# First token block of a spectral GLU kernel: tiles 4 to 7 transposed by VectorE blocks and a way through HBM instead of by TensorE

## The chip, the cores and the metric

One core of a Trainium2 chip runs the whole program. The metric is the device time of one execution in microseconds (us), the lower the better. A core has TensorE (matrix products, written PE in the profile, its weight loads PEld), VectorE (DVE), ScalarE (ACT), GpSimd (POOL) and SyncE (SP, which here only issues transfers). They run their own instruction streams in order and wait for each other by semaphores. On-chip memory is SBUF and, for TensorE's results, PSUM in banks of 128 x 512 numbers; HBM lies outside.

## The reference, cut to what matters

The input x has 2048 tokens of 640 features, in float32. First a layer norm, a two-dimensional real FFT, a product with a complex filter, the inverse FFT, and a residual sum; then a layer norm, a bilinear GLU and a second residual sum:

```
h   = x + irfft2(rfft2(layernorm(x)) * (w_r + 1j * w_i))
z   = layernorm(h)
out = h + ((z @ w_gate) * (z @ w_up)) @ w_down        # 640 -> 1728 -> 640
```

## The kernel before

Tokens are held in 16 tiles of 128 tokens (partitions) by 640 features, `X[0]` to `X[15]`. Both Fourier transforms are matrix products with tables. The GLU works on two token blocks of 8 tiles (1024 tokens) each; a block is split into two halves `sb` of 512 tokens: tiles 0 to 3 are half 0 and tiles 4 to 7 half 1 of the first block. Every product of the GLU is done in three matmuls on rounded numbers: an operand is stored as a high part (rounded) and a low part (the rest), and high x high, high x low and low x high are summed.

The gate and up weights are cut into 14 chunks. Chunks 0 to 11 are multiplied by a Strassen scheme (`strassen`), which needs sums and differences of quarters of z (`t12`, `t34`, made of `TJ`, the differences that `turn_lo` makes, and of `TJ["b"]`, copies of tiles 0 to 3). Chunks 12 and 13 are plain products in `gu(c, sb)`; in the first block they run first, so that TensorE has work while the Strassen operands are being made.

For a product, z must lie with features on partitions: each normalised tile must be transposed. The change touches how this is done for tiles 4 to 7.

The place is the loop `for t in range(NT)` near the end of the inverse transform. Its iteration t issues, in this order:

1. `turn_mm(k)` for k in `tside[t]`: TensorE's transposes (L811) of a normalised tile.
2. `unfold(t + 2)`: ScalarE copies a part of tile t+2's PSUM (`s`, L758); `turn_hi(k)` on ScalarE (L821 the high part, L825 the copy for Strassen); VectorE's sum and difference `q` (L766, L767), among which the small scale computations in `dside[t]` are spread; `turn_lo(k)` on VectorE (L829 the low part, L834 and L835 the Strassen differences); GpSimd's sums `yt` (L763, L771).
3. `id_mm(t + 3)` on TensorE, into a pair of PSUM banks `eo`.
4. `aside[t]` on ScalarE: squares for the variance, the inverse root (L223), `normalise(k)` (L799).
5. `is1_mm(t)` on TensorE (the second half of the inverse transform), into a pair of banks, `y`, or `eo` for t = 12; and for t = 13 `gu(13, 0)` behind it, which takes banks of `eo` over.
6. `acc(t)` on VectorE: adds the result to `X[t]` (L782, or L784 with a row sum for t below 8). acc(12) is issued in iteration 13, behind L767 of tile 15.

The scale r and shift b of a tile (L223 on ScalarE; L225, L215, L227, L792 on VectorE) are computed for groups of tiles: 0 to 2, 3 to 5, 6 and 7. For 6 and 7 this ends in iteration 13; normalise(6) stands in iteration 13, normalise(7) in 14.

Behind the loop tiles 6 and 7 are transposed (`transp`), then `gu(12, 0)` runs, `load_raw(0)` (L995, SP) fetches the weights of Strassen chunk 0 into a buffer that held the inverse transform's tables, and the first step of the GLU begins (the branch `p == 6`, `blk == 0`). It issues, in an order written out by hand: t1's and t2's high parts (ScalarE, L853) with `copies` (L1006 on ScalarE splits off the high part of chunk 0's weights, L1007 on VectorE the low part); `late` (the low part of the gate of chunk 13, L948); t1's and t2's low parts (VectorE, L853); `fifth((5, 6, 7))`, TensorE's transposes of the last 128 features of tiles 5 to 7 (L842), with their high and low parts (L844, L845); the gate of chunk 12 (L954, L955, L956); sums of weights (L1010 to L1013) with high and low parts (L1018, L1023); `gu(13, 1)`, its gate (L945 to L948), `t_rest` (L849), t34 (L864, L868), `gu(12, 1)`, and then `strassen`, chunk after chunk.

The order of each engine is the order of the code; SP's queue is too: a transfer that waits holds those behind it. Later in the kernel, for the second block, VectorE already transposes tiles in 32 x 32 blocks (L1406), and they go to HBM and back (L1409, L1399).

Of the kernel before, what the change touches and what calls it, by code (L numbers as in the profile page):

```python
# [27 lines left out]
PLAIN, MID = 5, 10  # L28
IPLAIN, IFAR = 5, 9
SUMS = 7  # L30
IPARTS = ((5, 4), (9, 3), (12, 4))
AGAIN = {0: (5, 3, "dC"), 1: (8, 2, "qt"), 4: (10, 3, 0), 7: (13, 3, 1)}
NR = 4
# [16 lines left out]
def f32(ap):  # L50
    return ap.bitcast(F32)
# [29 lines left out]
def tile_spectral_glu(ctx: ExitStack, tc: tile.TileContext, x, wre, wim, wgu, wlast, wdown, wdlast,  # L81
                      cc, ci, fmain, frem, imain, irem, mm, out):
    nc = tc.nc
# [7 lines left out]
    tt, act = nc.vector.tensor_tensor, nc.scalar.activation  # L91
# [22 lines left out]
    def wk(shape, name):  # L114
        return work.tile(shape, F32, tag="wk", name=name)
# [4 lines left out]
    def mmx(o, l, r, start, stop):  # L120
        nc.tensor.matmul(o, l, r, start=start, stop=stop, skip_group_check=True)  # L121
# [108 lines left out]
    SC = {}  # L230
# [548 lines left out]
    def acc(t, ps, total=None):  # L779
        xv = X[t].rearrange("p (a b) -> p a b", a=2)  # L780
        if total is None:
            tt(xv, ps[:, :, 0:320], xv, op=OP.add)  # L782
        else:
            nc.vector.scalar_tensor_tensor(xv, ps[:, :, 0:320], 1.0, xv, op0=OP.mult, op1=OP.add, accum_out=total)  # L784
# [9 lines left out]
            SC[t] = r[:, i:i + 1], b[:, i:i + 1]  # L794
        return fs, cs

    def normalise(t, z):
        Z[t] = z
        act(z, X[t], AF.Identity, bias=SC[t][1], scale=SC[t][0])  # L799

    PT = {}

    def turn_mm(t):
        if t < 5:
            ps = pair("y").rearrange("p a b -> p (a b)")
        else:
            ps = single()
        n = 5 if t < 5 else 4
        PT[t] = ps[:, 0:n * P].rearrange("p (k s) -> p k s", k=n)
        for k in range(n):  # L810
            nc.tensor.transpose(PT[t][:, k], Z[t][:, k * P:(k + 1) * P], ident)  # L811

    def turned(t, l):
        sb, i = divmod(t % 8, 4)
        return xt[:, sb, 0:5 if t < 5 else 4, l, i * P:(i + 1) * P], PT[t]

    TJ = {}

    def turn_hi(t):
        hi, pk = turned(t, 0)  # L820
        act(hi, pk, AF.Copy)  # L821
        if t == 0:
            TJ["b"] = home("dA", [P, 4, 4, P], "bt")
        if t < 4:
            act(TJ["b"][:, t], pk[:, 0:4], AF.Copy)  # L825

    def turn_lo(t):
        lo, pk = turned(t, 1)
        tt(lo, pk, f32(turned(t, 0)[0]), op=OP.subtract)  # L829
        if t % 8 >= 4:  # L830
            j = t % 4
            d = TJ[j] = wk([P, 4, P], "tj")
            b = TJ["b"][:, j]
            tt(d[:, 0:2], pk[:, 0:2], b[:, 0:2], op=OP.subtract)  # L834
            tt(d[:, 2:4], pk[:, 2:4], d[:, 0:2], op=OP.subtract)  # L835

    def fifth(ts):
        ps = single()
        sb, i = divmod(ts[0] % 8, 4)
        n = len(ts) * P  # L840
        for k, t in enumerate(ts):
            nc.tensor.transpose(ps[:, k * P:(k + 1) * P], Z[t][:, 512:640], ident)  # L842
        hi, lo = (xt[:, sb, 4, l, i * P:i * P + n] for l in range(2))
        act(hi, ps[:, 0:n], AF.Copy)  # L844
        tt(lo, ps[:, 0:n], f32(hi), op=OP.subtract)  # L845

    def t_rest(j):
        b = TJ["b"][:, j].rearrange("p (a k) n -> p a (k n)", a=2)
# [20 lines left out]

        return [high, low]  # L870

    def transp(t):
        turn_mm(t)
        turn_hi(t)
        turn_lo(t)

    PG = {}

    def gu(c, sb, which=(1, 0), ks=range(5)):
        if which[0] == 1:  # L880
            PG[c, sb] = [single() for _ in range(2 if c < NC - 1 else 1)] * 2
        w = W[c]
        if c < NC - 1:
            wv = w.rearrange("p l (m k f) -> p l m k f", m=2, k=5)
            sel = [(PG[c, sb][m], lambda l, k, m=m: wv[:, l, m, (k + 3) % 5]) for m in which]
        else:
            wv = w.rearrange("p l (k f) -> p l k f", k=5)
            sel = [(PG[c, sb][0], lambda l, k: wv[:, l, k])]
        for b, ww in sel:
            for k in ks:  # L890
                mmx(b, ww(0, k), xt[:, sb, k, 0], k == 0, False)
                mmx(b, ww(0, k), xt[:, sb, k, 1], False, False)
                mmx(b, ww(1, k), xt[:, sb, k, 0], False, k == 4)
# [10 lines left out]
    for ts in (range(3), range(3, 6), range(6, 8)):  # L904
        n, t0 = len(ts), ts[-1] + 1
        fs, cs = scale_shift(ts, [scrap] * n, total[:, ts[0]:t0])
        dside[t0].append(fs[0])
        t1 = ts[0] + 6 if n == 3 else t0 + 3
        dside[t1] += fs[1 + n:]
        dside[t1 + 1 + (n == 2)] += cs[1:]  # L910
        for i, t in enumerate(ts):
            (behind[t1 - n + i + 3] if t in (0,) else aside[t1 - n + i]).insert(0, fs[1 + i])
            aside[t + 7 + (t == 3)].append(lambda t=t: normalise(t, zb[:, t % 4]))
            tside[t + 9].append(t)
        aside[t1].append(cs[0])

    tside[NT - 1] = []
# [41 lines left out]
    for t in range(NT):  # L959
        for k in tside[t]:  # L960
            turn_mm(k)
        if t == NT - 3:
            unfold(t + 2, [], tside[t], [lambda: acc(t - 1, PY[t - 1])])
            for f in dside[t]:
                f()
        elif t + 2 < NT:
            unfold(t + 2, dside[t], tside[t])
        else:
            for k in tside[t]:
                turn_hi(k)  # L970
                turn_lo(k)
        if t + 3 < NT:
            id_mm(t + 3)
        for f in aside[t]:
            f()
        if t == NT - 3:
            is1_mm(t)
            ht = home("qm", [P, 8192], "ht", F32R)
            hop = cut(ht, 0, 7, 2, 512)
            t3 = [cut(ht, 7168, 2, 512), home("qt", [P, 2, 512], "t3", F32R)]  # L980
            banks("a", "pglu")
            gu(NC - 1, 0)
        else:
            is1_mm(t)
        if t != NT - 4:
            acc(t, PY[t], total[:, t:t + 1] if t < 8 else None)
        if t == NT - 2:
            late = gate_parts(NC - 1, 0)
    transp(6)
    transp(7)  # L990
    gu(NC - 2, 0)
    stage = home("stage", [P, 1448], "raw")

# [221 lines left out]
    for n, (blk, p) in enumerate(steps):  # L1215
        if p == 6:
            if blk == 0:
# [1 line left out]
                copies, sums, high, low = prep(0, blk, nc.vector)  # L1219
                TJ["12"] = home("qr", [P, 2, 2, 2, 512], "t12", F32R)  # L1220
                t1s = [t12(j) for j in range(4)]
                for j in range(3):
                    t1s[j][0]()
                copies()
                t1s[3][0]()
                late()
                t1s[0][1]()
                t1s[1][1]()
                t1s[2][1]()
                fifth((5, 6, 7))  # L1230
                wdn = load_d(p)
                t1s[3][1]()
                late = gate_parts(NC - 2, 0)
                sums()
                high()
                late()
                gu(NC - 1, 1)
                late = gate_parts(NC - 1, 1)
                for j in range(4):
                    t_rest(j)  # L1240
# [332 lines left out]
```

## Time and profile before

| | |
|---|---|
| median of 3 runs | 671.34 us (671.05 to 671.4) |
| the profiled execution | 671.31 us |
| its span, first to last instruction | 669.5 us |
| busy: TensorE, VectorE, ScalarE, GpSimd | 659.8, 469.1, 321.5, 393.3 us |
| granted TensorE clock over the span | 1.00 |

Times within the profile are us from the span's start. A timeline row gives start, length, engine, line, operation, the tile written and the tile read, their shapes and a count; rows of the same kind in a row are merged, their length is from the first start to the last end. In brackets stands how long the engine had been idle before it, and which instruction ended that. `e`, `y`, `eo` and `d` are PSUM banks, `zb` the normalised tiles, `xt` the transposed operand, `wst`, `wdir` weights.

### The profile page before, as it was taken

The page shows a single profiled execution, that of the slowest core. Times are in us where ns is not written, and L with a number is a line of the kernel's source. Part 1 is how long each engine was busy: PE and PEld are TensorE (multiplying, and loading weights), DVE is VectorE, ACT ScalarE, POOL GpSimd, SP SyncE. Part 2 cuts the span into 40 slices and gives each one's busy share as a digit, 9 for nine tenths or more (in the row PEclk, how much of TensorE's full clock was granted, in tenths as well). Part 3 has the DMA queues.
Part 4 walks back from the last instruction along what each step waited for, and adds up shares of the span by engine and source line. Part 5 has one row for each costly group of instructions (what it writes and reads, how often), then busy time and mean ns, then how long its engine had stood idle before and what let it go on. Part 6 is the DMA issues. An engine that isn't in the chain of part 4 may idle for free.

```text
span 669.5 us, 10243 instructions
## 1 busy us (share of the span) xinstructions
PE 659.8 (99%) x3695; PEld 587.1 (88%) x3695; DVE 469.1 (70%) x952; ACT 321.5 (48%) x622; POOL 393.3 (59%) x377
## 2 busy tenths in 40 slices
PE   6999999999999999999999999999999999999997
PEld 6999999888888888888888899888888888888887
DVE  6969997788767767594857567754757475757644
ACT  6977774585525243453626146534434251624220
POOL 3101124750397978969686445198786869697610
PEclk9999999999999999999999999999999999999999
DMA  8639885502212120142332467212011121212004
GB/s 319 227 107 283 245 246 157 163 1 80 78 40 80 39 79 33 28 99 60 98 79 84 93 134 260 79 41 78 12 35 73 41 78 40 79 40 80 1 0 158
DMA packets 48953, 66.12 MB, mean 99 GB/s; under 512 B 24082, under 2 KB 30670, under 8 KB 48774
## 3 DMA queue, kind: packets, MB, share of 16 engines
q1 hardware_dynamic: 48246, 62.91, 30.5%
q0 software_dynamic: 288, 2.16, 0.8%
q8 instruction: 29, 0.48, 0.3%
q10 hardware_dynamic: 368, 0.39, 0.2%
q14 instruction: 22, 0.18, 0.1%
HBM read 54.61 MB, written 10.84 MB: 98 GB/s over the span
## 4 chain that ended last, share of the span: by engine, by line
PE 95%; ACT 2%; DVE 1%; DMA 1%; issue 0%; DVEq 0%
PE e L121 50%; PE d L121 26%; PE eo L121 4%; PE y L121 2%; PE re L121 2%; PE u L476 2%; PE im L527 2%; PE im L121 2%; PE im L270 2%; PE ir L527 1%; DMA x<-in_x_dram 1%; ACT s L296 1%; ACT fold L212 0%; ACT fold L211 0%; PE y L811 0%; PE u L527 0%
## 5 line engine op out<-in xcount | busy, mean ns | idle before, releaser
L121 PE MATMUL e<-xt,wst 128*128 128x512 f32 x864 | 211.0, 390 | 0.0
L121 PEld LDWEIGHTS e<-xt,wst 128*128 128x128 f32 x864 | 160.7, 188 | 31.7
L1093 DVE TENSOR_TENSOR x<-d,x 128x320 f32<-128x320 f32 x280 | 120.5, 483 | 41.2 <-PE d L121 37.0
L121 PE MATMUL d<-wd,ht 128*128 128x320 f32 x832 | 142.1, 309 | 0.0
L121 PEld LDWEIGHTS d<-wd,ht 128*128 128x128 f32 x832 | 129.6, 188 | 5.1
L1007 POOL TENSOR_TENSOR wst<-raw,wst 128x1024 fp32r<-128x1024 f32 x23 | 55.4, 2410 | 69.9 <-ACT wst L1006 69.9
L121 PE MATMUL e<-t,wst 128*128 128x512 f32 x360 | 94.1, 391 | 0.0
L121 PEld LDWEIGHTS e<-t,wst 128*128 128x128 f32 x360 | 66.6, 188 | 13.3 <-ACT h L1147 0.3
L121 PE MATMUL d<-wt,ht 128*128 128x320 f32 x360 | 68.9, 309 | 0.0
L1023 POOL TENSOR_TENSOR wst<-raw,wst 128x896 fp32r<-128x896 f32 (+1 forms) x46 | 65.1, 1436 | 0.2 <-ACT wst L1018 0.2
L121 PEld LDWEIGHTS d<-wt,ht 128*128 128x128 f32 x360 | 57.3, 188 | 0.8
L1109 ACT ACTIVATE ht<-e 128x512 fp32r<-128x512 f32 x44 | 26.4, 600 | 50.0 <-DVE e L1171 24.1
L1018 ACT ACTIVATE wst<-raw 128x896 fp32r<-128x896 f32 (+1 forms) x48 | 30.1, 676 | 30.7 <-POOL raw L1012 30.0
L1167 DVE TENSOR_TENSOR e<-e,h 128x512 f32<-128x512 f32 x24 | 16.8, 699 | 39.2 <-ACT wst L1018 21.7
L1068 DVE TENSOR_TENSOR x<-d,x 128x320 f32<-128x320 f32 x62 | 27.5, 486 | 22.6 <-PE d L121 22.6
L687 ACT ACTIVATE wd<-draw 128x320 fp32r<-128x320 f32 (+1 forms) x30 | 15.7, 560 | 55.2 <-POOL draw L697 52.3
L121 PE MATMUL e<-xt,wdir 128*128 128x512 f32 x180 | 41.9, 392 | 0.0
L1147 ACT ACTIVATE h<-e 128x512 f32<-128x512 f32 x24 | 14.3, 596 | 56.7 <-PE e L121 56.7
L121 PEld LDWEIGHTS e<-xt,wdir 128*128 128x128 f32 x180 | 33.4, 188 | 7.5 <-ACT xt L821 0.5
L1112 DVE TENSOR_TENSOR ht<-e,ht 128x512 fp32r<-128x512 f32 x54 | 37.0, 686 | 1.6 <-ACT ht L1109 1.3
L1164 ACT ACTIVATE h<-e 128x512 f32<-128x512 f32 x24 | 14.4, 598 | 46.8 <-PE e L121 46.8
L666 POOL TENSOR_TENSOR wd<-draw,wd 128x640 fp32r<-128x640 f32 x8 | 12.4, 1577 | 40.8 <-ACT wd L665 40.8
(240 smaller groups left out, 1187.1 us busy)
## 6 DMA issues: line engine op xcount, KB each, us to landing
raw<-in_wgu_dram SPq DMA_DIRECT2D x24, 640.0 KB
draw<-in_wdown_dram SPq DMA_DIRECT2D x24, 320.0 KB
wts<-in_wre_dram SPq DMA_DIRECT2D x16, 322.0 KB
x<-in_x_dram SPq DMA_DIRECT2D x15, 320.5 KB
out_dram<-x SPq DMA_DIRECT2D x15, 320.0 KB
bits<-in_mm_dram SPq DMA_DIRECT2D x32, 128.0 KB
wts<-in_wim_dram SPq DMA_DIRECT2D x9, 322.0 KB
zfar<-zr SPq DMA_DIRECT2D x32, 80.0 KB
```

The costliest lines, as they stand in the source:

```text
L121: nc.tensor.matmul(o, l, r, start=start, stop=stop, skip_group_check=True)
L527: nc.tensor.matmul(out, y[:, h, a:b], inv(g, h), start=n == 0, stop=n == len(ys) - 1)
L687: act(o[:, 0, a:a + n], src, AF.Copy)
L1007: ptt(wa[:, 1], stage[:, 0:1024], f32(wa[:, 0]), op=OP.subtract)
L1018: act(ws[:, 0, o:o + b - a], stage[:, a:b], AF.Copy)
L1023: ptt(ws[:, 1, o:o + b - a], stage[:, a:b], f32(ws[:, 0, o:o + b - a]), op=OP.subtract)
L1068: tt(xv, ps[b][:, 0:320], xv, op=OP.add)
L1093: tt(xv, o, xv, op=OP.add)
L1109: act(hop[:, a, 0], src, AF.Copy)
L1112: engine.tensor_tensor(hop[:, a, 1], src, f32(hop[:, a, 0]), op=OP.subtract)
L1164: act(h1, oa, AF.Copy)
L1167: tt(ob, ob, h1, op=OP.add)
```

## The change

Tiles 0 to 3 are handled as before. For tiles 4 to 7:

- `normalise` writes its 640 features in another order: of each group of 160 features, five by 32, the blocks of 32 are brought together in such a way that a later copy can fetch whole runs.
- normalise(6) and (7) stand one iteration earlier (12 and 13), and so do the scale and shift of tiles 6 and 7 (iteration 12).
- `swap(ts)`, called at the end of iterations 11 (tile 4), 12 (tile 5) and 13 (tiles 6 and 7): VectorE transposes the tile in 32 x 32 blocks; SP writes it to HBM (320 KB, one transfer a tile); and SP reads it back in four transfers a tile, one for each group of 32 partitions, so that the blocks land where a full transpose would have them.
- `land_hi(t)` (ScalarE) makes the high part from that, `land_lo(t)` the low part on GpSimd and the two Strassen differences on VectorE. They are issued in iteration 14 for tile 4, in 15 for tile 5, and in the first GLU step for tiles 6 and 7.
- TensorE's transposes of tiles 4 to 7 and of the fifths, with their high and low parts, are gone.
- The first GLU step issues in another order, and `gu(13, 1)` runs all matmuls that need high parts of z first, then those that need low parts.

```diff
+SWAPS = {11: (4,), 12: (5,), 13: (6, 7)}
...
-    def normalise(t, z):
+    def normalise(t, z, mixed=False):
         Z[t] = z
-        act(z, X[t], AF.Identity, bias=SC[t][1], scale=SC[t][0])
+        i = X[t]
+        if mixed:
+            i, z = i.rearrange("p (k q b) -> p k q b", k=5, q=4), z.rearrange("p (q k b) -> p k q b", k=5, q=4)
+        act(z, i, AF.Identity, bias=SC[t][1], scale=SC[t][0])
...
     def turn_lo(t):
         lo, pk = turned(t, 1)
         tt(lo, pk, f32(turned(t, 0)[0]), op=OP.subtract)
-        if t % 8 >= 4:
-            j = t % 4
-            d = TJ[j] = wk([P, 4, P], "tj")
-            b = TJ["b"][:, j]
-            tt(d[:, 0:2], pk[:, 0:2], b[:, 0:2], op=OP.subtract)
-            tt(d[:, 2:4], pk[:, 2:4], d[:, 0:2], op=OP.subtract)
-
-    def fifth(ts):
...
+    zround = far.tile([4, P, D], F32, name="zround")
+    ZR, ZL = {}, {}
+
+    def swap(ts):
+        for t in ts:
+            r = ZR[t] = wk([P, D], "zs")
+            nc.vector.transpose(r, Z[t])
+        for t in ts:
+            nc.sync.dma_start(zround[t - 4], ZR[t])
+        for t in ts:
+            o = wk([P, D], "zl")
+            ZL[t] = o.rearrange("p (i k b) -> p k i b", i=4, k=5)
+            src = zround[t - 4].rearrange("(i a) (q x) -> q a i x", i=4, q=4)
+            for q in range(4):
+                nc.sync.dma_start(o[32 * q:32 * q + 32].rearrange("p (i x) -> p i x", i=4), src[q])
+
+    def split4(ap):
+        return ap.rearrange("p k (i b) -> p k i b", i=4)
+
+    def land_hi(t):
+        act(split4(xt[:, 1, :, 0, (t - 4) * P:(t - 3) * P]), ZL[t], AF.Copy)
+
+    def land_lo(t):
+        hi, lo = (xt[:, 1, :, l, (t - 4) * P:(t - 3) * P] for l in range(2))
+        nc.gpsimd.tensor_tensor(split4(lo), ZL[t], split4(f32(hi)), op=OP.subtract)
+        j = t - 4
+        d = TJ[j] = wk([P, 4, P], "tj")
+        tt(split4(d[:, 0:2]), ZL[t][:, 0:2], split4(TJ["b"][:, j, 0:2]), op=OP.subtract)
+        tt(split4(d[:, 2:4]), ZL[t][:, 2:4], split4(d[:, 0:2]), op=OP.subtract)
...
-    def gu(c, sb, which=(1, 0), ks=range(5)):
+    def gu(c, sb, which=(1, 0), ks=range(5), late=False):
...
+            if late:
+                for l, m in ((0, 0), (1, 0), (0, 1)):
+                    for k in ks:
+                        mmx(b, ww(l, k), xt[:, sb, k, m], l + m + k == 0, m == 1 and k == 4)
+                continue
...
-        dside[t1 + 1 + (n == 2)] += cs[1:]
+        dside[t1 + 1] += cs[1:]
         for i, t in enumerate(ts):
             (behind[t1 - n + i + 3] if t in (0,) else aside[t1 - n + i]).insert(0, fs[1 + i])
-            aside[t + 7 + (t == 3)].append(lambda t=t: normalise(t, zb[:, t % 4]))
-            tside[t + 9].append(t)
+            aside[t + 7 + (t == 3) - (n == 2)].append(lambda t=t: normalise(t, zb[:, t % 4], t >= 4))
+            if t < 4:
+                tside[t + 9].append(t)
...
         if t != NT - 4:
             acc(t, PY[t], total[:, t:t + 1] if t < 8 else None)
+        if t in SWAPS:
+            swap(SWAPS[t])
+        if t >= NT - 2:
+            land_hi(t - 10)
+            land_lo(t - 10)
         if t == NT - 2:
             late = gate_parts(NC - 1, 0)
-    transp(6)
-    transp(7)
     gu(NC - 2, 0)
...
                 t1s = [t12(j) for j in range(4)]
-                for j in range(3):
-                    t1s[j][0]()
+                t1s[0][0]()
+                t1s[1][0]()
+                land_hi(6)
                 copies()
-                t1s[3][0]()
+                land_hi(7)
                 late()
+                land_lo(6)
                 t1s[0][1]()
                 t1s[1][1]()
+                land_lo(7)
+                t1s[2][0]()
+                t1s[3][0]()
                 t1s[2][1]()
-                fifth((5, 6, 7))
                 wdn = load_d(p)
                 t1s[3][1]()
                 late = gate_parts(NC - 2, 0)
                 sums()
                 high()
                 late()
-                gu(NC - 1, 1)
+                gu(NC - 1, 1, late=True)
```

More of the change, by code (lines that the diff above doesn't have):

```diff
@@ L795, in scale_shift @@
         return fs, cs
-    def normalise(t, z):
+    def normalise(t, z, mixed=False):
         Z[t] = z
-        act(z, X[t], AF.Identity, bias=SC[t][1], scale=SC[t][0])
+        i = X[t]
+        if mixed:
+            i, z = i.rearrange("p (k q b) -> p k q b", k=5, q=4), z.rearrange("p (q k b) -> p k q b", k=5, q=4)
+        act(z, i, AF.Identity, bias=SC[t][1], scale=SC[t][0])
     PT = {}
     def turn_mm(t):
[L804 to L810, printed above, removed]
+        PT[t] = pair("y").rearrange("p a b -> p (a b)")[:, 0:D].rearrange("p (k s) -> p k s", k=5)
+        for k in range(5):
             nc.tensor.transpose(PT[t][:, k], Z[t][:, k * P:(k + 1) * P], ident)
     def turned(t, l):
-        sb, i = divmod(t % 8, 4)
-        return xt[:, sb, 0:5 if t < 5 else 4, l, i * P:(i + 1) * P], PT[t]
+        return xt[:, 0, :, l, t * P:(t + 1) * P], PT[t]
     TJ = {}
@@ L823, in turn_hi @@
             TJ["b"] = home("dA", [P, 4, 4, P], "bt")
-        if t < 4:
-            act(TJ["b"][:, t], pk[:, 0:4], AF.Copy)
+        act(TJ["b"][:, t], pk[:, 0:4], AF.Copy)
     def turn_lo(t):
@@ L829, in turn_lo @@
         tt(lo, pk, f32(turned(t, 0)[0]), op=OP.subtract)
-        if t % 8 >= 4:
-            j = t % 4
-            d = TJ[j] = wk([P, 4, P], "tj")
-            b = TJ["b"][:, j]
-            tt(d[:, 0:2], pk[:, 0:2], b[:, 0:2], op=OP.subtract)
-            tt(d[:, 2:4], pk[:, 2:4], d[:, 0:2], op=OP.subtract)
-    def fifth(ts):
[L838 to L845, printed above, removed]
+    zround = far.tile([4, P, D], F32, name="zround")
[23 more added lines that the diff above has]
+        tt(split4(d[:, 2:4]), ZL[t][:, 2:4], split4(d[:, 0:2]), op=OP.subtract)
     def t_rest(j):
@@ L870, in t34 @@
         return [high, low]
[L872 to L875, printed above, removed]
     PG = {}
-    def gu(c, sb, which=(1, 0), ks=range(5)):
+    def gu(c, sb, which=(1, 0), ks=range(5), late=False):
         if which[0] == 1:
@@ L909, in tile_spectral_glu @@
         dside[t1] += fs[1 + n:]
-        dside[t1 + 1 + (n == 2)] += cs[1:]
+        dside[t1 + 1] += cs[1:]
         for i, t in enumerate(ts):
             (behind[t1 - n + i + 3] if t in (0,) else aside[t1 - n + i]).insert(0, fs[1 + i])
-            aside[t + 7 + (t == 3)].append(lambda t=t: normalise(t, zb[:, t % 4]))
-            tside[t + 9].append(t)
+            aside[t + 7 + (t == 3) - (n == 2)].append(lambda t=t: normalise(t, zb[:, t % 4], t >= 4))
+            if t < 4:
+                tside[t + 9].append(t)
         aside[t1].append(cs[0])
-    tside[NT - 1] = []
     raw0 = home("dA", [P, 3, D], "raw0")
@@ L967, in tile_spectral_glu @@
             unfold(t + 2, dside[t], tside[t])
[L968 to L971, printed above, removed]
         if t + 3 < NT:
```

## The prediction

> **What bounds the kernel now.** I read the page first, for the engine with no room, and then the timeline of each engine around the change (140 to 180 us).
>
> ```profile
> PE 659.8 (99%) x3695; PEld 587.1 (88%) x3695; DVE 469.1 (70%) x952; ACT 321.5 (48%) x622; POOL 393.3 (59%) x377
> PEclk9999999999999999999999999999999999999999
> PE 95%; ACT 2%; DVE 1%; DMA 1%; issue 0%; DVEq 0%
> ```
>
> TensorE is busy 99% of the span and carries 95% of the chain that ended last. Behind the change it never idles again, so what it loses there arrives at the end undiminished, and so does what it saves. Its timeline through the change (start, length; the pitch is the distance between starts):
>
> ```profile
> 147.81 1.28 PE L121 MATMUL eo<-yt,tab 128*128 128x320 f32 x4
> 148.92 0.71 PE L811 MATMUL y<-ident,zb 128*128 128x128 f32 x5
> 149.47 1.24 PE L121 MATMUL y<-yt,tab 128*128 128x320 f32 x4
> 150.70 3.65 PE L121 MATMUL e<-xt,wdir 128*128 128x512 f32 x15
> 154.19 0.60 PE L811 MATMUL e<-ident,zb 128*128 128x128 f32 x4
> 154.62 2.32 PE L121 MATMUL y<-yt,tab 128*128 128x320 f32 x8
> 156.78 1.04 PE L811 MATMUL e<-ident,zb 128*128 128x128 f32 x8
> 157.57 7.21 PE L121 MATMUL e<-xt,wdir 128*128 128x512 f32 x30
> 164.62 0.49 PE L842 MATMUL e<-ident,zb 128*128 128x128 f32 x3
> 164.87 10.47 PE L121 MATMUL e<-xt,wdir 128*128 128x512 f32 x45
> 175.18 1.52 PE L121 MATMUL e<-xt,wst 128*128 128x512 f32 x6
> 176.54 1.52 PE L121 MATMUL e<-t,wst 128*128 128x512 f32 x6
> ```
>
> In order: is1_mm(12), tile 4's transposes, is1_mm(13), gu(13,0) at 150.70, tile 5's, is1_mm(14) and (15), tiles 6 and 7, gu(12,0), the fifths, gu(13,1) with gu(12,1), and the first Strassen products.
>
> **What it removes.** The four L811/L842 groups, by the distance to the next start: 0.55 + 0.43 + 0.79 + 0.25 = 2.0 us. That is the most that can be won: 669.3.
>
> **What it adds on VectorE at once.** A block transpose of a 128x640 tile is in the trace, much later:
>
> ```profile
> L1406 DVE STREAM_TRANSPOSE zr<-z x8: 834/836/845, 291.9 to 369.9; 128x640 f32<-128x640 f32 x8
> ```
>
> 0.84 us, with a pitch near 0.77. Tile 4's goes between acc(11) and the unfolding of tile 14. VectorE there, and the two ScalarE rows that matter:
>
> ```profile
> 146.69 0.48 DVE L766 TENSOR_TENSOR q<-eo,s 128x322 f32<-128x322 f32 x1
> 147.09 0.48 DVE L767 TENSOR_TENSOR q<-eo,s 128x322 f32<-128x322 f32 x1
> 147.72 0.82 DVE L829 TENSOR_TENSOR xt<-y,xt 128x640 fp32r<-128x640 f32 x1
> 148.93 0.49 DVE L766 TENSOR_TENSOR q<-eo,s 128x322 f32<-128x322 f32 x1 [0.38 <-ACT s L758]
> 149.34 0.48 DVE L767 TENSOR_TENSOR q<-eo,s 128x322 f32<-128x322 f32 x1
> 149.74 0.82 DVE L782 TENSOR_TENSOR x<-eo,x 128x640 f32<-128x640 f32 x1
> ```
>
> ```profile
> 147.57 0.92 ACT L799 ACTIVATE zb<-x,b,r 128x640 f32<-128x640 f32 x1
> 148.39 0.44 ACT L758 ACTIVATE s<-eo 128x322 f32<-128x322 f32 x1
> ```
>
> *Step 1.* L767 of tile 14 ends at 148.3 instead of 147.57. is1_mm(12) writes into the pair of banks that L767 frees, so it starts near 148.45 instead of 147.81: 0.6 lost, just what dropping tile 4's transposes gives back (0.55). TensorE is through is1_mm(13) at 150.7, as now.
>
> *Step 2.* gu(13,0) starts now at 150.70, 0.14 after acc(12) (149.74 + 0.82) ends: it waits for it. acc(12) stands behind L766/L767 of tile 15 on VectorE, these wait for ScalarE's copy s (L758, the 0.38 above), and s now has normalise(6) ahead of it in ScalarE's order, as the change puts both normalise(5) and normalise(6) into iteration 12. normalise(6) needs its scale and shift, which VectorE makes after L829 of tile 3: w and times first, L829 at about 148.65, r at 149.4, b. r has a trap:
>
> ```profile
> 142.12 0.75 POOL L771 TENSOR_TENSOR yt<-q 128x318 f32<-128x318 f32 x1
> 142.19 0.69 DVE L227 SCALAR_TENSOR_TENSOR r<-w,r 128x3 f32<-128x3 f32 x1
> ```
>
> An instruction on three columns took 0.69 and ended as GpSimd's did. The same pair of GpSimd sums runs here until about 150.0 (two of 0.75 behind 148.4). So b is ready near 150.4, normalise(6) runs to 151.2 (0.82 pitch by the two rows above), s to 151.7, L766 and L767 (0.41 each) to 152.5, acc(12) to 153.3, gu(13,0) starts at 153.5: 2.8 later than now. What was hidden is now in line. Behind it tile 5 gives back 0.43, tiles 6 and 7 0.79, the fifths 0.25, and the wait inside gu(12,0) 0.2 (30 matmuls at 0.229, the pitch of the 45, need 6.9, not 7.05): TensorE alone stands 1.2 later at gu(13,1).
>
> **The way through HBM.** All of it is issued by SP, in order: write 4, four reads 4, write 5, four reads 5, writes 6 and 7, eight reads, and only then load_raw(0), which now is issued at 156.97. Each read group waits for its write to land, and holds everything behind it. Prices:
>
> ```profile
> 108.37 0.58 SPq L718 DMA_DIRECT2D ifar<-qr  x1
> 110.78 0.30 SPq L726 DMA_DIRECT2D xt<-ifar  x1
> ```
>
> ```profile
> 175.95 0.33 SPq L995 DMA_DIRECT2D raw<-in_wgu_dram  x1
> ```
>
> ```profile
> 179.74 1.06 ACT L1006 ACTIVATE wst<-raw 128x1024 fp32r<-128x1024 f32 x1 [0.17 <-DMA raw<-in_wgu_dram]
> ```
>
> ```profile
> L1399 SPq DMA_DIRECT2D z<-zfar x16: 302/427/599, 390.2 to 402.5; - x16
> ```
>
> From a write's issue to the read that waited for it: 2.4. From the issue of 640 KB of weights to the ScalarE instruction that waited for them: 3.8. Issue of a comparable read: 0.30 to 0.60, I take the median, 0.42. When a tile's last read lands no row shows: between 2.4 and 3.8 from its issue; I take 2.4, as 80 KB is nearer the small one. Then: write 4 at 147.6 (transpose done), reads 150.0 to 151.7; write 5, reads 154.1 to 155.8; writes 6 and 7; reads 158.2 to 161.5; weights issued at 161.5, there at 165.3. Tiles 6 and 7 land at 161.9 and 163.5: ahead of the weights. The dearest thing on this path is thus not the tiles but the weights behind them.
>
> **What is late next.**
>
> ```profile
> 161.52 1.04 ACT L1006 ACTIVATE wst<-raw 128x1024 fp32r<-128x1024 f32 x1
> ```
>
> ```profile
> 160.07 0.42 DVE L834 TENSOR_TENSOR tj<-e,bt 128x256 f32<-128x256 f32 x1
> ...
> 162.59 1.23 DVE L1007 TENSOR_TENSOR wst<-raw,wst 128x1024 fp32r<-128x1024 f32 x1 [0.26 <-ACT wst L1006]
> ...
> 166.38 0.55 DVE L845 TENSOR_TENSOR xt<-e,xt 128x384 fp32r<-128x384 f32 x1
> ```
>
> ```profile
> 175.63 0.58 ACT L954 ACTIVATE u<-e 128x512 f32<-128x512 f32 x1
> ```
>
> L1006 moves from 161.52 to 165.3, **3.8**. land_hi(7) is queued behind it on ScalarE (to 167.0), so gu(13,1) starts near 167.0, not 164.87. On VectorE L1007 heads a gapless row (t1 and t2 low parts, the gate, the sums, t_rest) that ends in t34's high parts and then L954, which frees the bank for the product at 176.54: 0.3 of slack only. Into this row the change puts the differences of tiles 6 and 7 (four of 0.42, formerly ahead of L1007) and takes L845 out (0.5): **1.2**. And the low parts on GpSimd meet it:
>
> ```profile
> 181.60 2.41 POOL L1007 TENSOR_TENSOR wst<-raw,wst 128x1024 fp32r<-128x1024 f32 x1
> ```
>
> ```profile
> 182.27 2.82 DVE L859 TENSOR_TENSOR xt<-bt,xt 128x1024 fp32r<-128x1024 f32 x1 [3.14 <-ACT xt L859]
> ```
>
> Of the same size as VectorE's L1007 (1.23), it took 2.82, ending 1.08 after GpSimd's. The Trainium skill (GPSIMD Engine Reference, "8. Key points") says that GpSimd shares its SBUF interfaces with VectorE, in contention with instructions of two SBUF inputs; this trace agrees, 2.82 against 1.23. A low part takes 2.41 x 640/1024 = 1.5; tile 7's runs from 167.6 to 169.1 and stands before tile 6's difference, due at 168.2: **0.9** (bounds: 0 and 1.5). TensorE's 1.2 and its wait for land_hi(7) run beneath this.
>
> Two edits I cost at nothing. The new order of gu(13,1) keeps its 15 matmuls; the ten that need high parts only take 2.3 and cover tile 7's low part (1.5). normalise with blocks reordered and the high parts from strided blocks get the price of plain 128x640 instructions; no row shows these patterns, and half a microsecond each would still be inside the range.
>
> Sum: 3.8 + 1.2 + 0.9 = 5.9 us. The profiled execution took 671.31 (span 669.5, 1.8 around it) beside a median of 671.34: 671.3 + 5.9 = **677.2**. Its own range: with 0.30 per read SP is 1.9 earlier and ScalarE's own order then holds L1006 at about 163.4, 3.9 in all, 675.2; with 0.60, 2.9 more, 680.1.
>
> **The rivals.** *A, hidden after all:* the transfers land before they are asked for and the order on ScalarE costs nothing, so 2.0 are won: **669.3**. For it: tiles 4 to 7 aren't read by TensorE before 164, over 10 us after the first normalise. Against it: the wait of gu(13,0) for acc(12), which has no slack now. *B, only the order:* SP is quick, GpSimd disturbs nobody. gu(13,0) is then 2.3 late (r without its 0.5), the gate behind it 2.3 - 0.43, ScalarE has one high part of 0.5 less before L1006: that is 1.4 late, with the 1.2 of the differences 2.6: **673.9**. *C, the clock:* TensorE would stand still for about 4 us before the product now at 176.54 (ready near 178.6, started near 182.5). If its granted clock fell to half there, 15 matmuls at 0.229 would cost 3.4 more: **680.6**. Against it: the clock row shows no slice below 9, though TensorE waits in the first slices of the span. The Trainium skill (TensorE: Matmul & The Clock Gate, "Why this matters for your kernels") warns of idle gaps over about 3 us; no stall here is so long, so no run here shows it. *D, one tensor:* if the slots of zround were held as one, write 5 and writes 6 would also wait for the reads before them to land, 2.0 each (2.4 less the 0.42 of its issue): 4.0 more, **681.2**. Between A and B a gain and a loss may cancel: about 671.
>
> **How the numbers follow.** Forecast 0.55; B 0.18; A 0.08; C 0.08; D 0.06; cancelling 0.05. About 0.2% (1.3 us) is what a measurement of this kernel can tell from no change. Faster is A, 0.08; same is the cancelling case, 0.05; slower the rest, 0.87. The range leaves out A, the cancelling case and D, 0.19: from 673.5, just under B, to 680.7, just over C.
>
> **What would show it.** Step 1: is1_mm(12) starts near 148.4. Step 2: normalise(6) ends after 150.5 ahead of s, acc(12) ends and gu(13,0) starts near 153.4. The HBM way: SP's load_raw(0) issued after 159, with all sixteen reads ahead of it, and L1006 waiting for a DMA. The row on VectorE: L1007 after 165, a difference of tile 6 that takes over 1 us beside GpSimd's low part, TensorE idle for some 4 us before the first product with t. It is wrong if gu(13,0) starts before 151.5, or if load_raw(0) is issued before 158.5 and L1006 doesn't wait for it.

## The result, and the profile after

| | before | changed |
|---|---|---|
| median | 671.37 us (671.05 to 671.45) | 679.55 us (678.02 to 680.09) |
| the profiled execution, its span | 671.31, 669.5 us | 680.09, 678.3 us |
| granted TensorE clock over the span | 1.00 | 0.995 |

The ratio is 1.0118, with a 95% interval of 1.0106 to 1.013: slower by 8.2 us. The forecast was 677.2, with a range of 673.5 to 680.7.

The page of the changed kernel, its engines, the granted clock in 40 slices, and the chain that ended last:

```profile
PE 662.4 (98%) x3675; PEld 588.1 (87%) x3675; DVE 469.2 (69%) x951; ACT 321.8 (47%) x621; POOL 400.2 (59%) x381
PEclk9999999998999999999999999999999999999999
PE 92%; ACT 2%; DMA 2%; DVE 2%; SPq 1%; issue 1%; POOL 0%; POOLq 0%; ACTq 0%; DVEq 0%
```

TensorE has 20 instructions fewer and 2.6 us more busy time. Its share of the chain fell from 95 to 92%, and one slice of the clock row shows an 8. TensorE's timeline through the change:

```profile
148.48 1.31 PE L122 MATMUL eo<-yt,tab 128*128 128x320 f32 x4 [0.48 <-DVE w L226]
149.63 1.24 PE L122 MATMUL y<-yt,tab 128*128 128x320 f32 x4
153.39 5.04 PE L122 MATMUL e<-xt,wdir 128*128 128x512 f32 x15 [2.51 <-DVE x L783]
160.18 7.22 PE L122 MATMUL e<-xt,wdir 128*128 128x512 f32 x30
168.50 10.52 PE L122 MATMUL e<-xt,wdir 128*128 128x512 f32 x45 [1.10 <-ACT xt L848]
183.42 2.78 PE L122 MATMUL e<-t,wst 128*128 128x512 f32 x6 [3.05 <-ACT u L965]
186.00 1.33 PE L122 MATMUL e<-xt,wst 128*128 128x512 f32 x3
190.61 1.62 PE L122 MATMUL d<-wd,ht 128*128 128x320 f32 x10
```

Besides 0.48 ahead of is1_mm(12), three new waits stand in it: 2.51 ahead of gu(13,0), 1.10 ahead of gu(13,1), 3.05 ahead of the first product with t. That product starts at 183.42 in place of 176.54, 6.88 later. The first down product (the row of `d`) starts at 190.61 in place of 181.98, 8.63 later. Of the kernel before, two rows further on:

```profile
177.90 0.84 PE L121 MATMUL e<-xt,wst 128*128 128x512 f32 x3
181.98 1.62 PE L121 MATMUL d<-wd,ht 128*128 128x320 f32 x10
```

So 1.75 more was lost between the two, where no wait is shown: six matmuls took 2.78 that took 1.52 before, and three took 1.33, not 0.84. gu(13,0), too, took 5.04 for 3.65. The windows view of the same trace (length, busy time of TensorE, its weight loads, VectorE, ScalarE and GpSimd, then the granted clock, DMA share, GB/s) shows why:

```profile
149.50:152.90 3.40, 1.38 (x6) 0.63 (x4) 2.68 (x6) 2.06 (x3) 0.68 (x2) 1.00 0.48 129
152.90:156.30 3.40, 2.91 (x7) 2.36 (x8) 2.55 (x4) 0.74 (x1) 2.80 (x3) 0.50 0.44 133
180.20:183.60 3.40, 0.35 (x2) 0.18 (x2) 3.37 (x6) 1.86 (x4) 0.00 (x0) 1.00 0.00 0
183.60:187.00 3.40, 3.40 (x9) 2.63 (x10) 2.65 (x5) 2.11 (x4) 1.31 (x1) 0.50 0.82 280
```

Twice the clock was granted at half for 3.41 us, each time behind a stretch of that length in which TensorE had worked for 1.38 and for 0.35 us.

What held the product with t, on ScalarE, on VectorE with GpSimd, and on SP:

```profile
150.27 0.92 ACT L803 ACTIVATE zb<-x,b,r 128x640 f32<-128x640 f32 x1 [1.75 <-DVE b L793]
151.10 0.42 ACT L759 ACTIVATE s<-eo 128x322 f32<-128x322 f32 x1
166.76 1.06 ACT L1016 ACTIVATE wst<-raw 128x1024 fp32r<-128x1024 f32 x1 [2.08 <-DMA raw<-in_wgu_dram]
167.72 0.72 ACT L848 ACTIVATE xt<-zl 128x640 fp32r<-128x640 f32 x1
182.79 0.58 ACT L965 ACTIVATE u<-e 128x512 f32<-128x512 f32 x1
```

```profile
149.26 0.72 DVE L228 SCALAR_TENSOR_TENSOR r<-w,r 128x2 f32<-128x2 f32 x1
152.43 0.81 DVE L783 TENSOR_TENSOR x<-eo,x 128x640 f32<-128x640 f32 x1
167.91 1.23 DVE L1017 TENSOR_TENSOR wst<-raw,wst 128x1024 fp32r<-128x1024 f32 x1 [4.63 <-ACT wst L1016]
169.86 0.98 DVE L855 TENSOR_TENSOR tj<-zl,bt 128x256 f32<-128x256 f32 x1
172.42 0.42 DVE L855 TENSOR_TENSOR tj<-zl,bt 128x256 f32<-128x256 f32 x1
```

```profile
168.52 2.04 POOL L852 TENSOR_TENSOR xt<-zl,xt 128x640 fp32r<-128x640 f32 x1 [2.19 <-ACT xt L848]
```

```profile
158.23 3.64 SPq L842 DMA_DIRECT2D zl<-zround  x8
161.97 0.38 SPq L1005 DMA_DIRECT2D raw<-in_wgu_dram  x1
```

SP issues the weights of chunk 0 at 161.97, behind all reads. ScalarE waits for them and starts L1016 at 166.76 (before 161.52: 5.24 later). VectorE stood idle for 4.63 and then runs its row, in which one difference beside GpSimd's low part takes 0.98 in place of 0.42. L965, which frees the bank for the product with t, starts at 182.79 (before 175.63: 7.16 later).

### The profile page after: what moved, and what is told of

It reads as the page before. It is cut to its first block, busy times and chain, and to the rows that moved or that the text cites. A ratio compares the mean times of both kernels' runs of the same rounds, so it can differ in the third digit from the quotient of the medians.

```text
span 678.3 us, 10255 instructions
## 1 busy us (share of the span) xinstructions
PE 662.4 (98%) x3675; PEld 588.1 (87%) x3675; DVE 469.2 (69%) x951; ACT 321.8 (47%) x621; POOL 400.2 (59%) x381
## 4 chain that ended last, share of the span: by engine, by line
PE 92%; ACT 2%; DMA 2%; DVE 2%; SPq 1%; issue 1%; POOL 0%; POOLq 0%; ACTq 0%; DVEq 0%
PE e L122 48%; PE d L122 26%; PE eo L122 4%; PE re L122 2%; PE u L477 2%; PE im L528 2%; PE y L122 2%; PE im L122 2%; PE im L271 2%; PE ir L528 1%; SPq L842 1%; DMA raw<-in_wgu_dram 1%; DMA x<-in_x_dram 1%; ACT s L297 1%; ACT fold L213 0%
## 5 line engine op out<-in xcount | busy, mean ns | idle before, releaser
L1017 POOL TENSOR_TENSOR wst<-raw,wst 128x1024 fp32r<-128x1024 f32 x23 | 55.5, 2413 | 71.5 <-ACT wst L1016 71.5
L122 PEld LDWEIGHTS e<-t,wst 128*128 128x128 f32 x360 | 67.3, 190 | 16.7 <-ACT u L965 3.5
L122 PE MATMUL e<-xt,wdir 128*128 128x512 f32 x180 | 43.8, 402 | 3.6 <-DVE x L783 2.5
L1177 DVE TENSOR_TENSOR e<-e,h 128x512 f32<-128x512 f32 x24 | 16.8, 699 | 39.4 <-ACT wst L1028 21.8
L1122 POOL TENSOR_TENSOR ht<-h,ht 128x512 fp32r<-128x512 f32 x14 | 18.1, 1298 | 25.7 <-ACT ht L1119 25.5
```

The source lines that it names most:

```text
L1017: ptt(wa[:, 1], stage[:, 0:1024], f32(wa[:, 0]), op=OP.subtract)
L1122: engine.tensor_tensor(hop[:, a, 1], src, f32(hop[:, a, 0]), op=OP.subtract)
L1177: tt(ob, ob, h1, op=OP.add)
```

## The experiments

All ratios are against the kernel before, run beside each kernel on the same chip (medians 671.22 to 671.39). Unless said otherwise a kernel is the changed one with one edit.

**The weights first.** The weights of chunk 0 are fetched at the end of iteration 12, into the buffer of the tables itself, ahead of tile 5's write.

```diff
+        if t == NT - 4:
+            nc.sync.dma_start(tab[:, 0:1280], wgu[0])
...
-    stage = home("stage", [P, 1448], "raw")
+    stage = tab
...
-                load_raw(0)
```

> One edit to the changed kernel: chunk 0's weights are loaded into the same buffer at the end of iteration 12, ahead of tile 5's write on SP, instead of behind all sixteen reads. Theory 1 (the end is set by SP's queue, then the weights, then VectorE's gapless row, then the product with t): L1016 no longer waits for a DMA but for ScalarE's own order behind land_hi(6), near 164.6 instead of 166.76, and the end moves 2.1 us earlier, from 679.5 to about 677.4. Theory 2 (TensorE's own stalls, from the order on ScalarE and VectorE, set the end and the transfers are hidden): no change, 679.5.

Measured: 679.53, ratio 1.0121 (1.0106 to 1.0136): nothing won. SP of this kernel, and ScalarE:

```profile
151.62 0.38 SPq L995 DMA_DIRECT2D tab<-in_wgu_dram  x1
152.09 0.38 SPq L836 DMA_DIRECT2D zround<-zs  x1
157.31 1.74 SPq L842 DMA_DIRECT2D zl<-zround  x4
```

```profile
164.98 0.74 ACT L848 ACTIVATE xt<-zl 128x640 fp32r<-128x640 f32 x1 [0.74 <-DMA zl<-zround]
165.63 1.04 ACT L1018 ACTIVATE wst<-tab 128x1024 fp32r<-128x1024 f32 x1
```

Tile 5's write, issued 0.47 behind the weights, let the reads go only 5.2 later (157.31 - 152.09), not 2.3 as with the change. The tiles are now what is late: the high part of tile 6 waits for its landing, and the weights' high part, for which no wait is shown, is queued behind it. It starts 1.13 earlier than with the change, and the product with t 0.66 earlier (182.76). Theory 1's 677.4 was missed. The time is that of theory 2, but not for its reason: the row did move, by less than the 2 us that lie between the executions of one kernel (678.02 to 680.09 with the change). One wait stands in the place of the other, and the prediction's "the dearest thing on this path is the weights" holds for this order of SP's queue alone.

**The order on ScalarE and VectorE.** normalise(6) stands behind the copy s of tile 15, and tile 5's block transpose behind acc(12), so that acc(12) doesn't wait for them.

```diff
-SWAPS = {11: (4,), 12: (5,), 13: (6, 7)}
+SWAPS = {11: (4,), 13: (6, 7)}
...
-            aside[t + 7 + (t == 3) - (n == 2)].append(lambda t=t: normalise(t, zb[:, t % 4], t >= 4))
+            (behind[NT - 1] if t == 6 else aside[t + 7 + (t == 3) - (n == 2)]).append(
+                lambda t=t: normalise(t, zb[:, t % 4], t >= 4))
...
             unfold(t + 2, [], tside[t], [lambda: acc(t - 1, PY[t - 1])])
             for f in dside[t]:
                 f()
+            swap((5,))
```

> One edit to the changed kernel: normalise(6) stands behind ScalarE's copy s of tile 15, and tile 5's block transpose behind acc(12), so neither is ahead of acc(12). Both theories: gu(13,0) starts near 151.8 instead of 153.39, and the first fall of the clock is gone, so TensorE stands some 3 us earlier at is1_mm(14). Theory 1: tile 5's write is 0.8 later, so SP's queue and the weights are about 0.6 later, and the end is too: about 680.1. Theory 2: the end moves with TensorE, 3 us earlier: 676.5.

Measured: 679.34, ratio 1.012 (1.0105 to 1.0135). TensorE of this kernel:

```profile
151.97 3.68 PE L122 MATMUL e<-xt,wdir 128*128 128x512 f32 x15 [0.99 <-DVE x L783]
169.52 12.35 PE L122 MATMUL e<-xt,wdir 128*128 128x512 f32 x45 [4.90 <-ACT xt L848]
184.38 1.66 PE L122 MATMUL e<-t,wst 128*128 128x512 f32 x6 [1.15 <-ACT u L966]
```

gu(13,0) starts 1.42 earlier, gu(12,0) 2.78 earlier, and the product with t 0.96 later, since the reads and the weights behind them move by the delay of tile 5's transpose. What TensorE lost early, step 2 of the prediction, does not set the end; theory 2's 676.5 is excluded. The end did not move by the 0.96, as theory 1 had it (680.1): here the clock falls at 166.7, inside the wait ahead of gu(13,1), and not behind the product with t, whose six matmuls take 1.66 and not 2.78.

**Both together**, with no other edit.

> Both edits, the early weights and the order. Theory 1: what is left before L1016 is tile 6's landing, near 163.5, so L1016 near 164 and the end 2.7 earlier than the changed kernel: 676.8. Theory 2: as with the order alone, 676.5; then the two edits don't differ, and the early weights alone bring nothing.

Measured: 678.77, ratio 1.0109 (1.0093 to 1.0124), 2 us above both theories, the product with t at 182.75, the same place as with the weights first: TensorE's early gain is lost again to the same landing. Its windows view is needed for the clock, below.

**No way through HBM.** Writes and reads are left out; the high and low parts are taken from the block-transposed tile itself. What is left out is the exchange of blocks among the four groups of partitions, so tiles 4 to 7 enter the products with their blocks in other places; the instructions on the engines are the same.

```diff
-            nc.sync.dma_start(zround[t - 4], ZR[t])
-        for t in ts:
-            o = wk([P, D], "zl")
-            ZL[t] = o.rearrange("p (i k b) -> p k i b", i=4, k=5)
...
+            ZL[t] = ZR[t].rearrange("p (i k b) -> p k i b", i=4, k=5)
```

> The changed kernel without the way through HBM: the writes and reads of tiles 4 to 7 are left out, and the high and low parts are made from the block-transposed tile itself, so half 1's operands hold blocks in the wrong places. Theory 1: the weights are issued when is1_mm(15) ends, near 160.2, and are there at 164.0; L1016 follows ScalarE's order near 164.4: 2.3 earlier, 677.2, with gu(13,0) still at 153.4. If the trip explained all of the loss, 673 or less. Theory 2: no change, 679.5.

Measured: 675.46, 675.60, 678.27 and 680.24, median 676.93, ratio 1.0074 (1.0053 to 1.0096). The four executions had granted clocks of 1.00, 1.00, 0.995 and 0.992: at full clock the change without its transfers still costs 4.1 us, so the trip through HBM does not explain all of the loss. The median is near theory 1's 677.2, but with 4.8 us between the executions that says little; the trace says more. In the profiled execution, the one of 680.24:

```profile
165.06 1.06 ACT L1009 ACTIVATE wst<-raw 128x1024 fp32r<-128x1024 f32 x1 [0.21 <-DMA raw<-in_wgu_dram]
```

L1009, the weights' high part, starts 1.70 earlier than with the change, and the product with t 1.54 earlier (181.88). From the start of that instruction to the product with t it is 16.7 with the change, 16.6 in the run on order, 16.8 here, and 15.0 before. (With the weights first it is 17.1, as the low part of the weights there met GpSimd itself and took 1.69 for 1.23.) So the row on VectorE that begins with the weights has the same length within 0.2 in these three, 1.6 more than before, and hands on each delay at its head.

**A mended order.** Scale, normalises and block transposes stand behind acc(12) and acc(13), the weights go first, and the reads are made for two tiles at a time (8, not 16).

```diff
+        if t == NT - 4:
+            nc.sync.dma_start(tab[:, 0:1280], wgu[0])
+        if t == NT - 3:
+            swap((6, 7))
+            fetch_back(4)
+            fetch_back(6)
...
+                copies()
+                late()
+                sums()
+                land_hi(4)
+                land_hi(5)
+                land_lo(4)
+                land_lo(5)
                 t1s[0][0]()
                 t1s[1][0]()
                 land_hi(6)
-                copies()
                 land_hi(7)
-                late()
-                land_lo(6)
...
```

> Theory: the way through HBM costs because of where its steps stand, not because it is a way through HBM. Here the scale of tiles 6 and 7, both their normalises and all four block transposes stand behind acc(12) and acc(13), the weights of chunk 0 go first on SP's queue into a buffer that is free earlier, and the reads are made for two tiles at a time (8 transfers, not 16). Expected: gu(13,0) starts at 150.5 to 151 as before (153.39 with the change), the last read lands by 162, gu(13,1) starts by 164, the first product with t near 175 (before 176.54, with the change 183.42), no fall of the clock, and a time of 669.5 to 671, at or up to 1.8 us under the kernel before. Rival, the way through HBM costs wherever it stands (landing behind the weights, low parts on GpSimd, longer VectorE row): 675 or more, with the product with t after 180.

Measured: 676.75, ratio 1.0084 (1.0069 to 1.0099). gu(13,0) started at 150.88 as expected, but the rest missed: the clock fell (gu(13,1) with gu(12,1) took 12.25), and the product with t came at 182.18, so that the rival's numbers (675 or more, after 180) came true. GpSimd and VectorE of this kernel:

```profile
162.33 3.36 POOL L853 TENSOR_TENSOR xt<-zb,xt 128x640 fp32r<-128x640 f32 x2 [10.69 <-ACT xt L849]
```

```profile
162.52 1.78 DVE L856 TENSOR_TENSOR tj<-zb,bt 128x256 f32<-128x256 f32 x1
164.33 1.64 DVE L857 TENSOR_TENSOR tj<-zb,tj 128x256 f32<-128x256 f32 x1
165.89 0.41 DVE L856 TENSOR_TENSOR tj<-zb,bt 128x256 f32<-128x256 f32 x1
```

Beside GpSimd's two low parts VectorE's differences took 1.78 and 1.64, each about as long as the low part beside it, and without them 0.41. Tiles 6 and 7 met the same (1.66 and 1.77). ScalarE's Strassen high parts waited for these differences, and the high parts of tiles 6 and 7 stood behind them, so gu(13,1) started at 168.74 after 5.22 of waiting. The collision that the prediction priced at 0.9 cost 0.56 in the changed kernel, where one pair met; here four meetings make VectorE's row 5.2 longer. The rival's reason, a cost wherever the way stands, is still not the right one: the runs below with all low parts on VectorE and with two tiles show it.

**The gap filled.** In the changed kernel the first Strassen product of chunk 0 (six matmuls) is done three times.

```diff
-            product(oa, True, wa, 384, b11)
+            for _ in range(3 if c == 0 and blk == 0 else 1):
+                product(oa, True, wa, 384, b11)
```

> The changed kernel, with the six matmuls of the first Strassen product of chunk 0 done three times in place of once, so that TensorE works (3.0 us of repeated work) in the 3.05 us in which it stood idle ahead of the first product with t. Theory, the clock falls because TensorE stood still: no fall to half at 183 to 187, the first product with t still at 183.4, and the end 1.2 to 1.7 us earlier in spite of more work, near 678.0. Rival, the clock falls for another reason (or what falls costs nothing at the end): the fall remains and the time is 679.5 or more.

Measured: 677.95, ratio 1.01 (1.0083 to 1.0117). Twelve matmuls more, and the median is 1.6 lower than that of the changed kernel; the two intervals overlap, so the trace has to tell it. TensorE, and the windows view:

```profile
153.05 3.68 PE L122 MATMUL e<-xt,wdir 128*128 128x512 f32 x15 [2.52 <-DVE x L783]
183.60 1.52 PE L122 MATMUL e<-t,wst 128*128 128x512 f32 x6
189.04 1.62 PE L122 MATMUL d<-wd,ht 128*128 128x320 f32 x10
```

```profile
165.60:169.00 3.40, 1.53 (x7) 1.19 (x7) 1.98 (x3) 1.69 (x2) 1.41 (x1) 1.00 0.26 100
169.00:172.40 3.40, 3.40 (x10) 2.70 (x9) 3.33 (x7) 0.64 (x1) 0.63 (x1) 0.51 0.02 5
183.60:187.00 3.40, 3.40 (x16) 2.82 (x15) 1.84 (x3) 3.20 (x6) 1.41 (x1) 1.00 0.95 347
```

The product with t starts 0.18 later than with the change, the down product 1.57 earlier: with the gap filled the clock stays at 1.00 there, and the six matmuls take 1.52. That is as the theory had it. What it had not: in this execution the clock fell at 169.0, behind a wait of 1.87, and not behind the wait of 2.52 at 153, behind which it had fallen with the change.

**The low parts on VectorE.** `nc.gpsimd.tensor_tensor` in `land_lo` becomes `tt`, nothing else.

> The changed kernel with the low parts of tiles 4 to 7 on VectorE in place of GpSimd. Theory: the meeting of both engines cost 0.56 us once (0.98 against 0.42), and two more 128x640 instructions of about 0.75 in VectorE's gapless row cost 1.5, so the product with t comes 0.9 us later than with the change, near 184.3, and the time is near 680.4. Rival, GpSimd's low parts hold VectorE up all along: the product with t comes earlier than 183.4 and the time is under 679.

Measured: 679.14, ratio 1.0119 (1.0104 to 1.0134). TensorE of this kernel:

```profile
173.20 9.84 PE L122 MATMUL e<-xt,wdir 128*128 128x512 f32 x35 [2.38 <-DVE xt L852]
184.24 1.55 PE L122 MATMUL e<-t,wst 128*128 128x512 f32 x6
```

The product with t came at 184.24, as expected. The time came out 1.3 lower than expected, though not as low as the rival's 679: TensorE now waits inside gu(13,1), for a low part, and not ahead of the product. The clock falls at 173.85, behind that wait, where TensorE is ahead of VectorE's row: its bank comes free at 184.02, and at half clock TensorE gets there only 0.2 later. Behind the product it stays at full clock.

**The mended order with all low parts on VectorE**, and the four high parts ahead of the Strassen high parts on ScalarE.

```diff
+                for t in range(4, 8):
+                    land_hi(t)
+                for t in range(4, 8):
+                    land_lo(t)
+                for t in range(4, 8):
+                    land_tj(t)
+                    t1s[t - 4][0]()
```

> The mended order (transposes and normalises behind acc(12), weights first, reads for two tiles at a time) with the four low parts on VectorE in place of GpSimd, and the four high parts ahead of ScalarE's Strassen high parts. Theory: in the mended order GpSimd's low parts stretched four of VectorE's differences from 0.42 to between 1.64 and 1.78, 5.2 us in its gapless row; on VectorE the four cost 4 x 0.75 = 3.0. So VectorE is 2.2 us earlier, no difference takes over 0.5, gu(13,1) starts near 165.5 (168.74), the product with t near 178 to 179 (182.18), and the time is 672.5 to 674.5 (676.75). Rival, the landing of the tiles from HBM is what holds gu(13,1): it still starts after 168, and the time stays at 676 or more.

Measured: 674.38, ratio 1.0049 (1.0035 to 1.0063), no difference over 0.43; gu(13,1) and the product with t came 0.5 later than expected. TensorE of this kernel:

```profile
165.95 12.14 PE L121 MATMUL e<-xt,wdir 128*128 128x512 f32 x45 [2.64 <-ACT xt L849]
179.53 1.67 PE L121 MATMUL e<-t,wst 128*128 128x512 f32 x6
```

So 5.2 of the 8.2 us was where the steps stood, in which order SP issued them and on which engine they ran. (From the mended order to this kernel two things change, the engine of the low parts and ScalarE's order; their shares are not told apart.) Nearly all of the 3.0 that remain is there by two ways at once. TensorE waits 2.64 for the landing, starts gu(13,1) 1.1 later than before, and loses 1.7 more as the clock falls behind that (12.14 for 10.47). VectorE, which has four block transposes more than before and its other work behind the landing, ends the last reading that the product waits for (L966) at 179.47.

**Two tiles only.** The kernel before, with tiles 6 and 7 alone on the way through HBM, the weights first, the low parts on VectorE; tiles 4 and 5 are transposed by TensorE.

> The kernel before with only tiles 6 and 7 on the way through HBM (block transposes on VectorE behind acc(13), weights of chunk 0 first on SP's queue, four reads for both tiles, low parts on VectorE); tiles 4 and 5 stay with TensorE. Theory: what VectorE's row can hold decides. Without the transposes of tiles 6 and 7 and two of the three fifths TensorE is 0.79 + 0.17 = 1.0 us shorter; VectorE has two block transposes (1.5) in its idle time ahead of 155.5 and no more work behind it than before. gu(13,0) starts at 150.7, gu(13,1) at 163.9 to 164.3, the product with t near 175.6 to 176.5 (before 176.54), no fall of the clock: 670.3 to 671.3. Rival, a way through HBM costs wherever it stands: 673 or more.

Measured: 671.15, ratio 0.9996 (0.9987 to 1.0005), and in a second measurement 670.95, ratio 0.9997 (0.9988 to 1.0006). What was expected of the second:

> The same kernel as two tiles through HBM, beside the one above on one chip: 671.0 to 671.3 if the time of the earlier call holds.

Its TensorE:

```profile
164.69 10.50 PE L121 MATMUL e<-xt,wdir 128*128 128x512 f32 x45 [0.79 <-ACT xt L870]
176.38 1.52 PE L121 MATMUL e<-t,wst 128*128 128x512 f32 x6
```

Here the time is that of the kernel before, so a way through HBM does not cost wherever it stands. Of the 1.0 that TensorE saves 0.8 goes into waiting for the landing.

**The scale first.** The same with the scale of tiles 6 and 7 ahead of tile 4's low part, and the block transposes ahead of acc(13).

```diff
-            unfold(t + 2, [], tside[t], [lambda: acc(t - 1, PY[t - 1])])
-            for f in dside[t]:
-                f()
+            unfold(t + 2, [], tside[t], [lambda: acc(t - 1, PY[t - 1])] + dside[t])
...
+        if t == NT - 3:
+            swap()
         if t != NT - 4:
             acc(t, PY[t], total[:, t:t + 1] if t < 8 else None)
```

> Two tiles through HBM as in the run before, with the scale and shift of tiles 6 and 7 on VectorE ahead of tile 4's low part and differences (1.65 of work) and the block transposes ahead of acc(13). Theory: the only thing that held TensorE there was the landing (0.79 idle ahead of gu(13,1)); now normalise(6) starts near 151.5 (152.77), the writes are issued near 153.6 (154.67), the high parts are done by 163.7, gu(13,1) starts at 163.9 to 164.1 (164.69) and the product with t near 175.7 (176.38): 670.3 to 670.7, 0.1 to 0.16% under the kernel before. Rival, something else then holds the product with t (the end of VectorE's row, the gate of chunk 12): 671.0 to 671.4 as before.

Measured: 670.59, as expected, ratio 0.9991 (0.9983 to 1.0), the product with t at 176.00 (175.7), and 0.38 of wait left ahead of gu(13,1). Its TensorE there:

```profile
164.33 10.48 PE L121 MATMUL e<-xt,wdir 128*128 128x512 f32 x45 [0.38 <-ACT xt L870]
```

It is the lowest time of all kernels here, 0.1% under the kernel before, with an interval that just reaches 1, so that a gain is not shown; the writes were issued at 154.14 and not 153.6, as GpSimd's sums held the scale up again (0.67 for one instruction on two columns).

## Why the prediction was right, and where not

The time lies in the range, 2.35 above the forecast. About 1.0 of that is the sum, 5.9 forecast and 6.9 measured at the product with t. The rest, about 1.3, is the clock, which the forecast had at nothing. The chain was foreseen; that the time lies in the range even so is owed to the room kept above the forecast, for slower reads (680.1) and for rival C, which had a chance of 0.08, and not to the sum.

*Step 1* was right: is1_mm(12) was due at 148.45 and started at 148.48, TensorE was through is1_mm(13) at 150.9 (150.7).

*Step 2* was right in each link: r held up by GpSimd's sum (0.72), normalise(6) to 151.2 ahead of s, acc(12) to 153.2, gu(13,0) at 153.39 (153.5). That it lies beneath the rest was right too, and the run on order shows it: TensorE earlier there, the end unchanged. Its price was mis-sized, as the clock fell at 152.9 and gu(13,0) took 1.4 longer.

*The way through HBM* was right in its order and in the trip: the reads were issued at 149.81, 153.98 and 158.23 (150.0, 154.1, 158.2), and the weights behind them at 161.97 (161.5).

*L1006 3.8 late* is the term that was mis-sized: L1016 was 5.24 late. 0.47 of the difference is SP's, since eight reads took 3.64 and not 3.3. 0.97 is the weights': 4.8 from issue to use in place of 3.8. That they stand behind 640 KB of reads can be at most half of that, as without any reads it was still 4.3 (165.06 - 160.77); what the rest is stays open.

*The differences, 1.2, and the collision, 0.9:* the second was 0.56, the first fits. 5.24 + 1.2 + 0.56 = 7.0 against 7.16 measured at L965. So the sum of 5.9 should have been 7.0, and the chain that it was made of was the right one. The runs with this order of VectorE's row (order, no way through HBM, and weights first but for its own meeting with GpSimd) show it: the product with t moves as the head of the row does.

*The two edits costed at nothing* were rightly so: normalise with its blocks reordered took 0.92, as plain, a high part from strided blocks 0.72 to 0.74, and gu(13,1) with gu(12,1) 10.52 for 10.47.

*"Behind the change it never idles again"* is nearly so. The 90 matmuls at the head of the second block take 20.42 to the next start before and with the gap filled, 20.83 with the change and 21.67 with the low parts on VectorE, where a wait of 0.69 is shown. What sets this is open, so a difference of some tenths between medians is weak evidence.

*Rival C, the clock,* came true beside the forecast, not in its place. Against it the prediction held that no slice of the row fell below 9 though TensorE waits early in the span. That step failed: what counts is how a wait lies on a grid of 3.41 us, and in the trace of before no stretch of that length on the grid was more than 47% idle (those at the very end left out). Its price, 3.4, was too high: 1.75 in the profiled execution, about 1.3 if the 6.9 of the product with t is taken from the 8.2 of the medians. It took 15 matmuls at half clock, some 6.9 us, and the fall lasted 3.41.

*The other rivals.* B was not tried as such; the run without transfers is its nearest, and at full clock it took 675.5, where B said 673.9. Its SP was quick, but the weights were issued only at 160.77, as TensorE was through is1_mm(15), which reads the tables in their buffer (158.42 + 2.32 = 160.74): step 2 and the queue were two reasons for the same delay, and the prediction had only the second. A (669.3) needed slack on VectorE that is not there; with two tiles the mended order comes to 0.2 to 0.6 us under the kernel before, with intervals that reach 1, with all four it stays 3 us above. D did not occur: the write of tile 5 was issued at 151.64, and ScalarE waited for tile 4's reads until 153.36.

## What to carry to other kernels

Work taken off the bounding engine is paid for on the engine that takes it: before a step is moved, look for the stretch where that engine is gapless and ends in something the bounding engine waits for, and count each instruction that the step adds there, including the time in which another engine's access to SBUF holds it up. In a queue that issues in order, ask of each transfer what stands behind it and of each edit which wait ends last next; taking away one such wait, or two, here moved the end by 0.8 us or less. And a new wait of TensorE of some 1.9 us or more can bring half clock for the matmuls behind it; as the traces here stand, that is 3.41 us at half for a step of the grid, some 1.7 lost, and nothing where TensorE is ahead of another engine.

## What the runs showed of the hardware

**The clock falls by a grid.** In the thirteen traces of this case the granted clock falls to half only for 3.413 us or twice that, and in each execution all falls lie on one grid of that step, whose place differs from one execution to the next (152.9 and 183.6 with the change: nine steps). Of 16 steps at half clock (those at the very end of an execution left out), 15 followed a step in which TensorE was idle for 55% or more; the sixteenth followed a step that was itself at half. No step with 47% or less was followed by a fall. So a wait as short as 1.87 us was enough where it lay within one step (the gap filled), and no fall followed waits of 2.52 (the gap filled) and 2.97 where the grid cut them in two. The run with both edits (weights first and order) shows that, its wait of 2.97 us cut at 166.4, the clock at 1.00 in all three steps:

```profile
163.00:166.40 3.40, 1.80 (x8) 1.15 (x7) 0.82 (x1) 2.01 (x3) 1.11 (x2) 1.00 0.74 175
166.40:169.80 3.40, 2.02 (x9) 1.68 (x10) 3.02 (x3) 1.04 (x2) 2.97 (x2) 1.00 0.58 193
169.80:173.20 3.40, 3.40 (x17) 2.81 (x16) 3.33 (x7) 1.18 (x3) 0.09 (x1) 1.00 0.02 5
```

This fits the spread of the run without transfers, 675.5 in one execution at clock 1.00 and 680.2 in another at 0.992, where three steps stood at half; the shorter execution has no trace, so for it that is not shown. The Trainium skill (TensorE: Matmul & The Clock Gate, "What's actually happening") has a free-running window of 3413 ns, and the falls agree with that; it lets the clock fall after an idle window, and here a window idle for little more than half was enough.

**A load ahead delays a small write's landing.** From the issue of a tile's write (320 KB) to the issue of the reads that waited for it 2.2 to 2.4 passed, and 5.2 with 640 KB of weights issued 0.47 ahead of it, 4.6 with the weights 0.86 ahead (both edits together).

**GpSimd and VectorE take turns.** A VectorE instruction with two operands in SBUF that starts while a GpSimd sum or difference runs ends 0.02 to 0.28 us after that ends: 1.78 for 0.42, 0.72 for 0.16, 0.98 for 0.42. The long one of the prediction (2.82 for 1.23) ends 1.08 after. Where VectorE is first, GpSimd's is the longer one: 2.04 for 1.57 beside L1017, which kept its 1.23. With one operand in PSUM no such thing is seen: L826 took 0.82 beside a GpSimd sum (148.51), as its like in the scale-first run took without one.
